# Output slices of the first block split as the others, the tail's counts moved forward, and a new order of the instructions

## The chip, the core and the metric

The kernel runs on one core of one Trainium2 chip. The metric is device time in microseconds (us) of one execution, taken on the chip. TensorE is called PE below, VectorE DVE, ScalarE ACT, GpSimd POOL, and SyncE, which issues most of the DMAs, SP.

## The reference, cut to what matters

Attention over 4 batches, 8 heads, 768 positions and 64 columns a head, in which a position sees the 96 positions behind it and 8 global ones, with a bias by distance; then a gated feed-forward of 3072 rows, 512 columns and 1536 hidden columns, whose weights come as float64.

```python
scores = scale * np.matmul(q, k.transpose(0, 1, 3, 2))
scores = scores + bias[None, :, :, :]
scores = np.where(keep, scores, -1000000000.0)
scores = scores - np.max(scores, axis=-1, keepdims=True)
a = np.exp(scores)
a = a / (np.sum(a, axis=-1, keepdims=True) + 1e-09)
attn_out = np.matmul(a, v).astype(np.float32)
...
x = np.ascontiguousarray(attn_out.transpose(0, 2, 1, 3)).reshape(B * S, H * D)
gate = 1.0 / (1.0 + np.exp(-(x @ w_gate)))
val = x @ w_val
return (gate * val @ w_out).astype(np.float32)
```

## The kernel before

The 3072 rows are eight blocks of three tiles of 128 rows. For block 0 the attention comes first; after that, the feed-forward of a block runs while the attention of the next is woven into it. A block's feed-forward is twelve slices (f0 to f11) of 128 hidden columns. `ff_in` makes a slice: twelve matmuls of 128x384 for the gate (`ps_g`), twelve for the value (`ps_u`), a tanh on ACT (L654), and the product on DVE. `ff_out` (L686) multiplies a slice with 512 columns of `w_out` for each of the three tiles, into three banks of PSUM that gather all twelve slices.

Float32 precision is had in two ways. A *split* operand is kept as a high part rounded to the type fp32r and a low part that is the rest; a product of two split operands is three fp32r matmuls (low x high, high x high, high x low). The gate and value matmuls are all of this kind (`w1h`, `w1l`, `xh`, `xl`). In `ff_out` it is so from slice f6 of block 0 on: the weights are split into `w2h` (ACT, L299) and `w2l` (a subtraction on POOL, L268) by `split_w2`, anew for each slice and into one buffer each; the hidden values into `hh` (ACT, L666) and `hl` (a subtraction on DVE, also recorded at L268). For the slices f0 to f5 of block 0, `UNSPLIT = 6`, DVE writes the product to `hh` at once (L660), nothing is split, and `ff_out` does one plain float32 matmul a tile, which stands in the trace as two records.

During block 0 the weights arrive: per slice two transfers of gate and value weights and one of `w_out`, as 64-bit numbers, from which ACT takes the mantissa bits (L280) and the top (L287), DVE joins them (L296; for `w_out` it also does the top, L289), ACT rounds `w1h` (L317) and POOL subtracts `w1l` in eight parts (L268).

The order of the instructions on each engine is written out by hand in the table `ORDER` for the first part of the program (on PE the first 1273 operations); what comes after is issued in the order that the scheduler chose. An engine runs its instructions in order, so one that waits holds up all behind it. SP's list sets the order of the transfers.

At the start PE does fourteen matmuls on zeros (`keep_busy`, L195), while the first q and k arrive and DVE builds the tables of distances (L220 to L230, L245). At the end the last tile is copied out of PSUM in halves, by DVE (L704) and then ACT (L705), and sent by a DMA of ACT's queue (L706). Behind `inner.close()` a check of the counts follows: the tiles `nf` and `wf` are allocated in `gpool`, in memory that was held by other tiles before; DVE computes them from `words` (L841 to L844), compares (L859, five times), reduces to one flag (L861), every engine loads the flag (L937) and branches (L938). The branch taken writes one element (L939); the other, a dense computation of everything anew, isn't run with these inputs.

Of the kernel before, what the change touches and what calls it, by code (L numbers as in the profile page):

```python
# [8 lines left out]
F32 = mybir.dt.float32  # L9
# [11 lines left out]
P = 128  # L21
# [86 lines left out]
def attn_moe_kernel(ctx, tc, qT, kT, v, counts, wg, wv, wo, out, B, H, S, D):  # L108
# [94 lines left out]
    make_identity(nc, ident)  # L203
    tabs = [cpool.tile([P, WIN], BF16, name=f"tab{h}") for h in range(H)]
    tabs0 = [cpool.tile([P, P], BF16, name=f"tabs{h}") for h in range(H)]
    nms = cpool.tile([P, 2 * (B * NTB * NPAIR) + 8], F32, name="nms")[:, :-8]
    def build_tables():

        nl, ng = low[:, 0:1], low[:, 1:2]
# [779 lines left out]
```

## Time and profile before

| | us |
|---|---|
| runs | 731.41, 732.67, 732.76 |
| median | 732.67 |
| profiled execution, its own time | 732.67 |
| its span | 730.9 |
| PE busy | 718.9 (98%) |
| DVE busy | 462.2 (63%) |
| ACT busy | 412.9 (56%) |
| POOL busy | 229.0 (31%) |

The span is the time from the first to the last record of the trace; the profiled execution's own time is 1.8 us above it. A share of busy time is an average over the whole program. The chain of waits is the sequence of work that ended last, followed back from the end; the view of windows gives busy time by stage; the waits of an engine name what it stood still for.

### The profile page before, as it was taken

What the parts mean: (1) busy time and instruction counts of PE and PEld (TensorE: products, weight loads), DVE (VectorE), ACT (ScalarE), POOL (GpSimd) and SP (SyncE); (2) the same over time, 40 slices, a digit from 0 to 9 for tenths busy, and PEclk for the clock granted to TensorE, in tenths of its full rate; (3) what the DMA queues carried; (4) which work ended last, traced back from release to release, by engine and by line L of the source; (5) the groups of instructions that cost most, each with busy time, mean ns of one, the idle gap of its engine ahead of it and who ended that gap; (6) DMA issues with size and microseconds to landing.
All of it is one profiled execution on the core that took longest, in us unless ns stands there. A gap on an engine that the chain in (4) does not pass through costs nothing.

```text
span 730.9 us, 12504 instructions
## 1 busy us (share of the span) xinstructions
PE 718.9 (98%) x4403; PEld 654.2 (90%) x4403; DVE 462.2 (63%) x1273; ACT 412.9 (56%) x938; POOL 229.0 (31%) x238
## 2 busy tenths in 40 slices
PE   8999999999999999999999999999999999999995
PEld 7777789989999899999999999999999999999994
DVE  6866664477777767777777777676787877221112
ACT  6777875656666545565565655565465755332222
POOL 4744665232322313232322223232223232212221
PEclk9999999999999999999999999999999999999998
DMA  7787542454354653444326343532335333010001
GB/s 236 237 285 266 190 154 79 110 106 89 84 137 84 149 102 69 98 117 96 61 64 146 77 107 75 89 102 63 91 82 111 87 61 56 15 44 1 1 0 47
DMA packets 136723, 74.27 MB, mean 102 GB/s; under 512 B 86992, under 2 KB 128976, under 8 KB 136656
## 3 DMA queue, kind: packets, MB, share of 16 engines
q1 hardware_dynamic: 136368, 73.17, 40.1%
q8 instruction: 36, 0.59, 0.3%
q14 instruction: 31, 0.25, 0.1%
q10 hardware_dynamic: 288, 0.26, 0.1%
HBM read 49.81 MB, written 6.29 MB: 77 GB/s over the span
## 4 chain that ended last, share of the span: by engine, by line
PE 95%; DMA 2%; DVE 1%; POOL 1%; ACT 1%; issue 0%; SPq 0%; DVEq 0%; ACTq 0%
PE ps_o L686 27%; PE ps_u L646 27%; PE ps_g L646 27%; PE ps_s L469 4%; PE ps_t L584 3%; PE ps_v L584 2%; PE ps_t L534 1%; PE ps_v L195 1%; DMA kr<-in_kT 1%; PE ps_s L455 1%; DMA turned<-halves 1%; POOL w2l L268 1%; PE ps_v L455 0%; DVE halves L549 0%; PE ps_o L610 0%
## 5 line engine op out<-in xcount | busy, mean ns | idle before, releaser
L268 POOL TENSOR_TENSOR w2l<-w2f,w2h 128x512 fp32r<-128x512 f32 x89 | 119.8, 1346 | 367.0 <-ACT w2h L299 361.2
L663 DVE SCALAR_TENSOR_TENSOR work<-work,ps_u 128x384 f32<-128x384 f32 x90 | 49.8, 553 | 140.9 <-PE ps_u L646 133.1
L646 PE MATMUL ps_g<-xh,w1l 128*128 128x384 f32 x384 | 131.8, 343 | 1.2 <-ACT work L654 1.2
L646 PE MATMUL ps_u<-xh,w1l 128*128 128x384 f32 x384 | 131.7, 343 | 0.2 <-DVE work L663 0.2
L646 PE MATMUL ps_g<-xl,w1h 128*128 128x384 f32 x384 | 130.0, 339 | 0.0
L646 PE MATMUL ps_g<-xh,w1h 128*128 128x384 f32 x384 | 129.7, 338 | 0.0
L646 PE MATMUL ps_u<-xl,w1h 128*128 128x384 f32 x384 | 129.3, 337 | 0.0
L646 PE MATMUL ps_u<-xh,w1h 128*128 128x384 f32 x384 | 129.3, 337 | 0.0
L666 ACT ACTIVATE hh<-work 128x384 fp32r<-128x384 f32 x90 | 47.0, 522 | 120.9 <-DVE work L663 120.6
L686 PE MATMUL ps_o<-w2l,hh 128*128 128x512 f32 x267 | 105.8, 398 | 0.8 <-POOL w2l L268 0.7
L686 PE MATMUL ps_o<-w2h,hh 128*128 128x512 f32 x267 | 103.9, 391 | 0.0
L686 PE MATMUL ps_o<-w2h,hl 128*128 128x512 f32 x267 | 103.3, 390 | 0.0
L501 ACT ACTIVATE work<-work,nms 128x256 f32<-128x256 f32 (+1 forms) x192 | 92.0, 481 | 12.4 <-DVE nms L488 11.8
L268 DVE TENSOR_TENSOR hl<-work,hh 128x384 fp32r<-128x384 f32 x90 | 73.3, 814 | 30.4 <-ACT hh L666 30.4
L299 ACT ACTIVATE w2h<-w2f 128x512 fp32r<-128x512 f32 x89 | 56.1, 631 | 59.0 <-PE ps_o L686 58.2
L646 PEld LDWEIGHTS ps_u<-xh,w1l 128*128 128x128 f32 x384 | 72.2, 188 | 5.1 <-issue 2.0
L646 PEld LDWEIGHTS ps_g<-xh,w1l 128*128 128x128 f32 x384 | 72.3, 188 | 4.8 <-ACT work L654 2.0
L654 ACT ACTIVATE work<-ps_g 128x384 f32<-128x384 f32 x96 | 46.6, 486 | 51.2 <-PE ps_g L646 48.4
L646 PEld LDWEIGHTS ps_g<-xl,w1h 128*128 128x128 f32 x384 | 72.2, 188 | 2.5 <-issue 1.1
L646 PEld LDWEIGHTS ps_u<-xl,w1h 128*128 128x128 f32 x384 | 72.2, 188 | 1.9 <-issue 0.2
L646 PEld LDWEIGHTS ps_g<-xh,w1h 128*128 128x128 f32 x384 | 72.2, 188 | 1.5 <-issue 0.5
L646 PEld LDWEIGHTS ps_u<-xh,w1h 128*128 128x128 f32 x384 | 72.2, 188 | 0.8
(125 smaller groups left out, 1178.9 us busy)
## 6 DMA issues: line engine op xcount, KB each, us to landing
qr<-in_qT SPq DMA_DIRECT2D x56, 192.0 KB, 3.4
kr<-in_kT SPq DMA_DIRECT2D x32, 192.0 KB, 2.7
raw<-in_w_gate SPq DMA_DIRECT2D x12, 512.0 KB, 4.8
raw<-in_w_val SPq DMA_DIRECT2D x12, 512.0 KB, 5.8
v<-in_v SPq DMA_DIRECT2D x32, 192.0 KB, 3.4
raw<-in_w_out SPq DMA_DIRECT2D x12, 512.0 KB, 4.0
out<-ost SPq DMA_DIRECT2D x23, 256.0 KB, 2.2
v<-in_v SPq DMA_DIRECT2D x16, 144.0 KB, 3.4
```

Source lines behind the costliest of these rows:

```text
L195: ins = nc.tensor.matmul(idle[:, 0:P], zeros.to_broadcast([P, P]), zeros.to_broadcast([P, P]), start=True, stop=True)
L268: eng.tensor_tensor(out, a, b, op=ALU.subtract)
L299: ins = nc.scalar.activation(hi, w, AF.Copy)
L455: ins = nc.tensor.matmul(ps[j][:, :w], st["qr"][hd, 0, qc], st["kr"][hd, k0:k0 + w], start=True, stop=True)
L469: nc.tensor.matmul(ps[j][:, :w], st["qs"][:, j, hl, qc], st["ks"][:, j, k0:k0 + w], start=(hl == 1), stop=(hl == 0),)
L501: ins = nc.scalar.activation(sb[:, j, :w], sb[:, j, :w], AF.Exp, scale=-1.0, bias=nm[:, j:j + 1], accum_out=sm[:, j:j + 1])
L584: ins = nc.tensor.matmul(av[j * D:(j + 1) * D, t * P:(t + 1) * P], vt[:, t, j * D:(j + 1) * D], st["pT"][t][:, m * j + c], start=(c == 0), ...
L646: nc.tensor.matmul(ps[:, :n], wt[f][:, i, c], xt[:, c, :n], start=(k == 0), stop=(k == 3 * NC - 1))
L654: last_gate[:] = [nc.scalar.activation(a[:, :n], ps[:, :n], AF.Tanh, scale=0.5)]
L663: nc.vector.scalar_tensor_tensor(a[:, :n], a[:, :n], 1.0, pss[1][:, :n], op0=ALU.add, op1=ALU.mult)
L666: nc.scalar.activation(hh[:, :n], a[:, :n], AF.Copy)
L686: ins = nc.tensor.matmul(outs[bi][t], ht[:, t * P:(t + 1) * P], wt, start=(f == 0 and k == 0), stop=(f == NF - 1 and k == len(parts) - 1),)
```

## The change

Four things change.

- `UNSPLIT` goes from 6 to 0: the slices f0 to f5 of block 0 split their weights and hidden values as all the others. Eighteen float32 matmuls become fifty-four fp32r ones; ACT gets six more `w2h` and six more `hh`, POOL six more `w2l`, DVE six more `hl`.
- `nf` and `wf` lie in eight spare columns of the tile `nms`, which is kept through the whole program. So their operations can stand in DVE's list near the start.
- The last tile is copied once, by ACT, and sent by ACT's queue as before.
- All five lists of `ORDER` are new; PE's names 1307 operations in place of 1273. Behind the lists, the order of PE, DVE, ACT and POOL is the same as before, up to the tail.

```diff
@@ ORDER
     tensor=(
-        "0-9 14-17 11 10 13 12 21 27 20 18-19 26 53 33 52 32 22 28-31 23-25 46-51 59 58 34 36-45 54-57 35 65 64 85 60-63 "
+        "0-9 14-15 11 13 10 21 12 20 18 16 19 27 22-23 33 26 53 32 24-25 28-31 17 46-52 59 58 36-45 34-35 54-57 85 65 64 "
...
-    nms = cpool.tile([P, 2 * (B * NTB * NPAIR) + 8], F32, name="nms")[:, :-8]
+    nms = cpool.tile([P, 2 * (B * NTB * NPAIR) + 8], F32, name="nms")
+    nf, wf = nms[:, -8:-6], nms[:, -6:].rearrange("p (w k) -> p w k", k=2)
+    nms = nms[:, :-8]
...
-    UNSPLIT = 6
+    UNSPLIT = 0
...
-                if t == nt - 1 and end:
-                    y, z = slice(0, DM // 2), slice(DM // 2, DM)
-                    nc.vector.tensor_scalar(ot[:, y], outs[bi][t][:, y], 0.5, None, op0=ALU.mult)
-                    nc.scalar.activation(ot[:, z], outs[bi][t][:, z], AF.Copy, scale=0.5)
-                    nc.scalar.dma_start(out[bass.ds(row, P), :], ot)
-                    continue
                 if t == 1 and end:
                     nc.vector.tensor_scalar(ot, outs[bi][t], 0.5, None, op0=ALU.mult)
                 else:
                     nc.scalar.activation(ot, outs[bi][t], AF.Copy, scale=0.5)
-                nc.sync.dma_start(out[bass.ds(row, P), :], ot)
+                (nc.scalar if end and t == nt - 1 else nc.sync).dma_start(out[bass.ds(row, P), :], ot)
...
-    nf = gpool.tile([P, 2], F32, name="nf")
-    wf = gpool.tile([P, 3, 2], F32, name="wf")
```

The table's numbers don't tell what moved; the orders do, at three places. In their rows a name carries the number of its buffer, and a line of after is 3 to 5 away from that of before.

PE at the start of the program, before: the matmuls on zeros (L195), then the first scores (L455) and transposes (L534).

```order
L195 MATMUL ps_v_100<-zeros_98 128x128 x14
L455 MATMUL ps_s_213<-kr_172,qr1_170 128x128
L455 MATMUL ps_g_214<-kr_172,qr1_170 128x128
L455 MATMUL ps_u_223<-kr_172,qr1_170 128x256
L455 MATMUL ps_o1_224<-kr_172,qr1_170 128x256
L455 MATMUL ps_s_243<-kr_172,qr1_170 128x256
L455 MATMUL ps_u_269<-kr_182,qr1_180 128x128
L455 MATMUL ps_g_244<-kr_172,qr1_170 128x256
L534 MATMUL ps_t_238<-ident_94,work_217 128x128 x2
```

The same place after.

```order
L198 MATMUL ps_v_100<-zeros_98 128x128 x12
L460 MATMUL ps_s_213<-kr_172,qr1_170 128x128
L460 MATMUL ps_u_223<-kr_172,qr1_170 128x256
L460 MATMUL ps_g_214<-kr_172,qr1_170 128x128
L460 MATMUL ps_s_243<-kr_172,qr1_170 128x256
L460 MATMUL ps_o1_224<-kr_172,qr1_170 128x256
L460 MATMUL ps_g_244<-kr_172,qr1_170 128x256
L539 MATMUL ps_t_238<-ident_94,work_217 128x128
L198 MATMUL ps_v_100<-zeros_98 128x128
L539 MATMUL ps_t_238<-ident_94,work_217 128x128
L460 MATMUL ps_u_269<-kr_182,qr1_180 128x128
```

Twelve matmuls on zeros stand ahead of the first scores in place of fourteen, and the scores of the second pair (`kr_182`) have moved behind the transposes of the first.

ACT about the first slices of block 0, before: the rounding of the weights (`w1h`), the tanh of f0 (`work_640`), the exponentials of the next block's attention (L501), and the bits of the next weights.

```order
L618 COPY hl_582<-ps_o2_575 128x384
L626 ACTIVATE xh_168<-hh_584 128x384
L280 ACTIVATE w2f1_157<-raw1_588 128x512
L317 ACTIVATE w1h1_133<-bits_597 128x1024
L654 ACTIVATE work_640<-ps_g_627 128x384
L501 ACTIVATE work_605,sm_606<-work_605,nms_131 128x256 x2
L514 ACTIVATE sm_606<-sm_606 128x2
L280 ACTIVATE bits_646<-raw0_593 128x1024
L287 ACTIVATE top_648<-raw0_593 128x1024
L501 ACTIVATE work_615,sm_616<-work_615,nms_131 128x256 x2
L317 ACTIVATE w1h2_134<-bits_646 128x1024
```

The same place after.

```order
L304 ACTIVATE w2h_677<-w2f0_156 128x512
L623 COPY hl_582<-ps_o2_575 128x384
L631 ACTIVATE xh_168<-hh_584 128x384
L322 ACTIVATE w1h1_133<-bits_597 128x1024
L285 ACTIVATE w2f1_157<-raw1_588 128x512
L506 ACTIVATE work_605,sm_606<-work_605,nms_131 128x256
L659 ACTIVATE work_640<-ps_g_627 128x384
L506 ACTIVATE work_605,sm_606<-work_605,nms_131 128x256
L519 ACTIVATE sm_606<-sm_606 128x2
L506 ACTIVATE work_615,sm_616<-work_615,nms_131 128x256
L671 ACTIVATE hh_673<-work_640 128x384
L285 ACTIVATE bits_646<-raw0_593 128x1024
```

The rounding of f0's `w_out` (`w2h_677`) now comes ahead of `w1h1`, and the rounding of its hidden values (`hh_673`) between the exponentials and the bits of f2.

DVE at the end of the program, before, from the last product on.

```order
L663 SCALAR_TENSOR_TENSOR work_8112<-work_8112,ps_u_8114 128x384
L268 TENSOR_TENSOR hl_8129<-work_8112,hh_8128 128x384
L709 TENSOR_SCALAR ost_8157<-ps_o1_7665 128x512
L704 TENSOR_SCALAR ost_8160<-ps_o2_7666 128x256
L841 CAST wf_8171<-words_91 128x2x2
L842 TENSOR_SCALAR wf_8171<-wf_8171 128x2
L843 TENSOR_TENSOR wf_8171<-wf_8171 128x2
L844 SCALAR_TENSOR_TENSOR nf_8170<-wf_8171 128x2
L859 TENSOR_SCALAR top_8176<-nf_8170 1x1 x4
L861 TENSOR_REDUCE flag_8186<-top_8176 1x1
L937 TENSOR_LOAD flag_8186
L938 COMPARE_AND_BRANCH
```

The same place after.

```order
L668 SCALAR_TENSOR_TENSOR work_8190<-work_8190,ps_u_8192 128x384
L273 TENSOR_TENSOR hl_8207<-work_8190,hh_8206 128x384
L708 TENSOR_SCALAR ost_8235<-ps_o1_7743 128x512
L934 TENSOR_LOAD flag_8261
L935 COMPARE_AND_BRANCH
```

The second copy of the last tile and the nine small operations are gone from here: four of the counts and four compares stand near the start, and the reduction to the flag (after L858) among the last block's slices. On SP the load of the flag stands ahead of the last five output transfers, and on ACT behind the last copy and its DMA.

## Rows read from the trace of the kernel before

**Rows 1.** The page: span, busy time by engine, and the chain's shares by engine.

```profile
span 730.9 us, 12504 instructions
PE 718.9 (98%) x4403; PEld 654.2 (90%) x4403; DVE 462.2 (63%) x1273; ACT 412.9 (56%) x938; POOL 229.0 (31%) x238
PE 95%; DMA 2%; DVE 1%; POOL 1%; ACT 1%; issue 0%; SPq 0%; DVEq 0%; ACTq 0%
```

**Rows 2.** The chain of waits from 715 us: start, duration, what.

```profile
723.04 0.43 DVE ost L704
723.50 0.39 ACT ost L705
723.92 2.06 DMA out<-ost
...
727.54 0.54 DVEq L937
...
728.24 0.54 issue
...
728.86 0.06 DVE top L939
```

**Rows 3.** The timeline from 719 us: start, duration, operation, idle before and releaser.

```profile
721.26 0.39 PE L686 MATMUL ps_o<-work,hl 128*128 128x512 f32 x1
...
721.68 0.60 ACT L711 ACTIVATE ost<-ps_o 128x512 f32<-128x512 f32 x1 [1.92 <-PE ps_o L686]
...
722.62 0.39 PE L686 MATMUL ps_o<-work,hl 128*128 128x512 f32 x1
...
726.20 0.17 DVE L841 CAST wf<-words 128x4 f32<-128x4 int32 x1 [2.73 <-DMA out<-ost]
```

**Rows 4.** The timeline of PE from 40 us: unsplit output matmuls, two records each.

```profile
40.95 1.02 PE L686 MATMUL ps_o<-w2f,hh 128*128 128x512 f32 x2
...
49.51 1.88 PE L686 MATMUL ps_o<-w2f,hh 128*128 128x512 f32 x4
```

**Rows 5.** The chain of waits from 290 us: nine split output matmuls in a row.

```profile
302.35 2.04 PE ps_o L686 x9
```

**Rows 6.** Windows: each engine's busy time (and its count), clock, DMA share, GB/s.

```profile
6.60:16.40 9.80, 9.05 (x78) 6.16 (x76) 7.72 (x36) 8.47 (x29) 5.34 (x8) 1.00 0.89 277
...
36.00:87.00 51.00, 51.00 (x278) 37.67 (x277) 31.78 (x77) 40.99 (x81) 27.00 (x54) 1.00 0.76 259
87.00:130.00 43.00, 43.00 (x259) 37.80 (x259) 24.73 (x60) 30.17 (x64) 24.24 (x36) 1.00 0.39 124
```

**Rows 7.** The page's costliest groups: the four operations that the split adds.

```profile
L268 POOL TENSOR_TENSOR w2l<-w2f,w2h 128x512 fp32r<-128x512 f32 x89 | 119.8, 1346 | 367.0 <-ACT w2h L299 361.2
...
L666 ACT ACTIVATE hh<-work 128x384 fp32r<-128x384 f32 x90 | 47.0, 522 | 120.9 <-DVE work L663 120.6
...
L268 DVE TENSOR_TENSOR hl<-work,hh 128x384 fp32r<-128x384 f32 x90 | 73.3, 814 | 30.4 <-ACT hh L666 30.4
L299 ACT ACTIVATE w2h<-w2f 128x512 fp32r<-128x512 f32 x89 | 56.1, 631 | 59.0 <-PE ps_o L686 58.2
```

**Rows 8.** Waits of ACT from 36 to 87 us: total, times, longest; first and last.

```profile
ACT w1h L317 <- DVE rc L518: 2.9, 2, 1.5
...
ACT bits L280 <- DMA raw<-in_w_val: 0.5, 1, 0.5
```

**Rows 9.** Waits of PE from 100 to 722 us: total, times, longest; two of three.

```profile
PE ps_g L646 <- ACT work L654: 1.2, 2, 0.8
PE ps_o L686 <- POOL w2l L268: 0.7, 2, 0.6
```

**Rows 10.** The chain of waits from the start to 36 us.

```profile
1.00 5.73 PE ps_v L195 x28
...
11.23 5.21 DMA kr<-in_kT
```

**Rows 11.** The view of the tile `hl`: shortest, median and longest subtraction in ns.

```profile
L268 DVE TENSOR_TENSOR hl<-work,hh x90: 543/559/1905, 84.8 to 719.8; 128x384 fp32r<-128x384 f32 x90
```

129 rows, old and new, of tables (gpsimd, scalar, sync, tensor) are left out of this document.

## The prediction

> **What bounds the kernel now.** I read the page first, then the chain of waits. PE is busy for 718.9 of 730.9 us and makes up 95% of the chain [rows 1]: between the first scores and the last output matmul nearly every saving must be one on PE itself, or a wait of PE that goes. Two places are different. At the end, the chain leaves PE at about 723.0 us and needs another 7.9 us for copies, one DMA, the check of the counts and a branch [rows 2]. At the start, 5.7 us are matmuls on zeros, and one transfer of k holds the chain until 16.4 us [rows 10]. So I take the change in three places (end, PE's work in block 0, start), and then ask which other engine is close enough to PE to spoil it. The windows show one: from 36 to 87 us, where block 0 runs f0 to f6 while the weights arrive, ACT is busy for 41.0 of 51.0 us, against 30.2 of 43.0 in the stretch behind [rows 6].
>
> The profiled execution took 732.67 us, which is the median of the three runs too; it is its span of 730.9 and 1.8 us around it. I sum against 732.67.
>
> **The end.** Before: the last matmul starts at 722.62; DVE copies one half at 723.04, ACT the other at 723.50 (0.39), the DMA goes at 723.92 and takes 2.06, to 725.98 [rows 2, 3]. Only then does DVE begin the counts: L841 sat idle for 2.73 us and its releaser is that DMA [rows 3], since `nf` and `wf` take over memory of the output tile. From there L841 to L861, the load of the flag (0.54), the branch (0.54) and L939 run to 728.92 [rows 2], and the span ends 2.0 us later at 730.9.
>
> After: one ACT copy. Tile 0's copy tells its price: its last matmul starts at 721.26, the copy at 721.68, and it takes 0.60 [rows 3]. So the copy runs from 722.62 + 0.42 = 723.04 to 723.64, the DMA goes at 723.67 and lands at 725.73, 0.25 earlier than before. The counts, the compares and the flag are long done. The loads of the flag and the branches stand behind the last work of each engine; ACT's are the latest: behind its DMA at 723.67 and some 0.4 us of issuing, 0.54 for the load and 0.6 for the branch make 725.2, half a microsecond before the landing. They are covered by the transfer; if that cover were gone, they'd cost up to 1.4 us. What is late next is the landing itself, and then the closing. Before, the closing took 2.0 us behind L939; if all of it comes behind the landing the span ends at 727.7 (a gain of 3.2), and if half of it has run by then at 726.7 (4.2). The chain of waits doesn't say what part waits for DMAs; I take 1.7 us, thus 727.4: **−3.5 us**, with 1.8 (loads and branches not covered) and 4.2 as ends.
>
> **PE's work in block 0.** An unsplit output matmul is two records. One takes 1.02 us, and two in a row 1.88 [rows 4], so one more costs 0.86. Nine split ones in a row take 2.04 us [rows 5], 0.227 each, and three of them 0.68. Eighteen matmuls thus save 18 x (0.86 − 0.68) = **−3.2 us**. All this lies on PE, which is the bound there (51.0 of 51.0 busy [rows 6]). The ends are 2.5 and 4.0, since single matmuls carry a change of operand shape in or out that the new order may add or save.
>
> **What the split adds elsewhere.** By the page's means [rows 7]: on ACT six times 0.631 + 0.522 = 6.9 us; on POOL six times 1.346 = 8.1; on DVE six times 0.814 = 4.9. In the window 36 to 87 us, which shrinks to 47.8, DVE comes to 31.8 + 4.9 = 36.7 and POOL to 27.0 + 8.1 = 35.1, both with more than 11 us to spare. ACT, with the first `w2h` ahead of the window (it stands in front of `w1h1`), comes to 41.0 + 6.3 = 47.3 of 47.8: full. It covers its extra work only by giving up its own waits. These were 10.2 us there in six rows, from 2.9 for DVE's `rc` to 0.5 for a transfer of weights [rows 8]. They are mostly the waits of an engine that is ahead, and PE didn't stand still behind them: it was busy for 51.00 of 51.00 us [rows 6]. Queued behind an ACT that waits are the tanh, on which PE's next gate bank depends, `hh`, on which the output matmuls depend, and `w1h`, on which POOL's `w1l` and PE's next slice depend. No row shows how much of this reaches PE. The bounds are 0 (all hidden, as before) and 47.3 + 10.2 − 47.8 = 9.7 us (no wait gives way). Behind 87 us ACT has 30% to spare and catches up. I take **+1.0**, near the lower end, since that is the nearest row: PE's waits for ACT after 100 us, where split slices run as well, are 1.2 us in all, in two waits [rows 9].
>
> **The start.** Two matmuls fewer on zeros ahead of the first scores are four records of 5.73/28 = 0.20 us, so up to 0.8 us earlier. PE is busy for 9.05 of 9.80 us between 6.6 and 16.4 [rows 6], so waits of 0.75 could go as well; the transfer of k that ended one at 16.4 was issued at 11.23 behind a 512 KB transfer of weights and took 5.2 [rows 10], and now it is issued ahead of that one. Against it: eight small DVE operations of 0.17 [rows 3] come in among the tables, 1.4 us at most, on which POOL's tables and the first softmax wait. Bounds −1.6 and +1.4; I take **−0.6**, as the new places of the scores and the transfers are on the side of the gain, and DVE has work for 7.72 of those 9.80 us.
>
> **The rest.** The two extra matmuls on zeros among the transposes, the new places of the same work in the lists, and the counts at the start change no amount of work; the order behind the lists is as before. I put them at nothing: where PE is never idle, order alone costs nothing (that PE comes some 4 us earlier to the later blocks is rival 2).
>
> Sum: 732.67 − 3.5 − 3.2 − 0.6 + 1.0 = 726.4 us.
>
> **Rival 1, slower: ACT becomes the bound from 36 to 87 us.** For it: 47.3 of 47.8 us with no room for a wait, in an order in which a wait for a transfer or for DVE's `bits` holds the tanh too. Against it: PE was busy for all of the 51.0 us while ACT waited 10.2, so ACT's lateness of that size was hidden by work done ahead, and such a lead is used up first. Its price is 9.7 us at most: 732.67 − 3.5 − 3.2 − 0.6 + 9.7 = 735.1. It decides the sign when over 7.3 of the 10.2 us of waits stay; with half of them, 5, the time is 730.4.
>
> **Rival 2: the later stalls grow.** PE arrives earlier at blocks whose transfers and POOL work are timed by others. Its waits from 100 to 722 us are 1.2 for ACT and 0.7 for POOL, and 0.2 more [rows 9]. As much again gives 726.4 + 2.1 = 728.5. Against it: the waits are single events, and PE was the bound around them.
>
> **Rival 3: POOL's subtractions block DVE's.** `hl` takes 0.559 us at the median and 1.905 at the longest [rows 11], and its mean of 0.814 [rows 7] says that a fifth or so of them are stretched by the 1.35 us between these two. POOL would be busy for 35.1 of 47.8 us in the window, so four of the six new `hl` may meet it: 5.4 us on DVE, which its spare 11 us can hold; if half of that reaches the matmuls that read `hl`, it is 2.7 and the time 729.1. The Trainium skill has the rule on the page "SBUF — State Buffer", section "Who interferes with whom": a DVE instruction with two inputs in SBUF and a GpSimd instruction that reads SBUF exclude each other, and the later one blocks fully. By that rule the cost of a meeting is the rest of the other's instruction, and the longest `hl` agrees with it.
>
> **Rival 4: the start or the end gives nothing.** If the eight operations and the new order of POOL's tables cost the start 1.4 us in place of the gain of 0.6, and the branches cost the end 1.0, the time is 726.4 + 2.0 + 1.0 = 729.4. The DMA's end behind the last matmul can't be gained away, but neither is it made longer.
>
> **How the numbers follow.** The forecast of 726.4, with its own ends at 723.4 (the large ends of the gains at the end and the start: 0.7 and 1.0, and no stall: 1.0, with 0.3 taken off since they won't all fall together) and 728: chance 0.62. Rival 1: 0.14, of which 0.04 lies above 734.1 and 0.04 between 731.2 and 734.1. Rival 2: 0.10. Rival 3: 0.07. Rival 4: 0.07. 0.2% of 732.67 is 1.5 us, about what a measurement of this kernel can tell from no change. Slower by more than that: 0.05 (rival 1, and a mixture of the others); within it: 0.05; faster: 0.90. The range reaches from 723.4 to 731.0, which leaves out the worse half of rival 1 and a start and end that are better than counted.
>
> **What would show it.** In the profile after: the last DMA's landing at about 718.5 on a span of 724.6, with no DVE operation behind it but L936, and 1.7 us to the end; the record count of `ps_o<-w2f,hh` at zero and PE busy for some 3 to 4 us less; the first scores near 6 us; ACT above 95% from 36 us to the end of f5, and PE's waits for ACT, `w1l` or `hl` before 90 us at about 1 us in all. I'm wrong if PE stands still for several microseconds in f0 to f6, if the closing waits for something that I don't see, or if the first scores don't move.

## The result: 723.55 us, 1.2% faster than before

The changed kernel took 723.55 us (median of four runs, 723.22 to 724.73); four runs of the kernel before beside it took 732.68 (731.41 to 732.76). The ratio is 0.9882, with a 95% interval of 0.9865 to 0.9899: faster by 9.1 us, where 6.3 were forecast. The time lies inside the range and close to its low end.

The page after: span, busy time by engine, and the four groups that the split adds to (a group is line, engine, operation, count | busy us, mean ns of one | idle time before, its releaser).

```profile
span 723.0 us, 12575 instructions
PE 714.1 (99%) x4421; PEld 659.1 (91%) x4421; DVE 467.2 (65%) x1278; ACT 418.3 (58%) x950; POOL 239.1 (33%) x244
...
L273 POOL TENSOR_TENSOR w2l<-w2f,w2h 128x512 fp32r<-128x512 f32 x95 | 129.4, 1363 | 370.8 <-ACT w2h L304 359.7
L671 ACT ACTIVATE hh<-work 128x384 fp32r<-128x384 f32 x96 | 50.1, 522 | 120.5 <-DVE work L668 120.2
L273 DVE TENSOR_TENSOR hl<-work,hh 128x384 fp32r<-128x384 f32 x96 | 77.8, 810 | 30.3 <-ACT hh L671 30.1
L304 ACT ACTIVATE w2h<-w2f 128x512 fp32r<-128x512 f32 x95 | 59.9, 630 | 56.9 <-PE ps_o L691 56.1
```

Each group has grown by six [rows 1, 7], at nearly the same price for one: ACT, POOL and DVE work 5 to 10 us longer, PE 4.8 us less. This execution took 724.73 us by its own time, the slowest of its four; a second profiled one (`again`, below) took 723.36, and where two executions of one kernel differ I show both.

### The profile page after: what moved, and what is told of

Read it like the earlier page. It is cut to its first block, busy times and chain, and to the rows that moved or that the text cites. A ratio compares the mean times of both kernels' runs of the same rounds, so it can differ in the third digit from the quotient of the medians.

```text
span 723.0 us, 12575 instructions
## 1 busy us (share of the span) xinstructions
PE 714.1 (99%) x4421; PEld 659.1 (91%) x4421; DVE 467.2 (65%) x1278; ACT 418.3 (58%) x950; POOL 239.1 (33%) x244
## 5 line engine op out<-in xcount | busy, mean ns | idle before, releaser
L273 POOL TENSOR_TENSOR w2l<-w2f,w2h 128x512 fp32r<-128x512 f32 x95 | 129.4, 1363 | 370.8 <-ACT w2h L304 359.7
L668 DVE SCALAR_TENSOR_TENSOR work<-work,ps_u 128x384 f32<-128x384 f32 x96 | 53.1, 553 | 137.8 <-PE ps_u L651 130.1
L671 ACT ACTIVATE hh<-work 128x384 fp32r<-128x384 f32 x96 | 50.1, 522 | 120.5 <-DVE work L668 120.2
L691 PE MATMUL ps_o<-w2l,hh 128*128 128x512 f32 x285 | 112.0, 395 | 1.1 <-ACT hh L671 1.0
L691 PE MATMUL ps_o<-w2h,hh 128*128 128x512 f32 x285 | 111.0, 391 | 0.0
L691 PE MATMUL ps_o<-w2h,hl 128*128 128x512 f32 x285 | 109.7, 391 | 0.0
L273 DVE TENSOR_TENSOR hl<-work,hh 128x384 fp32r<-128x384 f32 x96 | 77.8, 810 | 30.3 <-ACT hh L671 30.1
L304 ACT ACTIVATE w2h<-w2f 128x512 fp32r<-128x512 f32 x95 | 59.9, 630 | 56.9 <-PE ps_o L691 56.1
L659 ACT ACTIVATE work<-ps_g 128x384 f32<-128x384 f32 x96 | 46.6, 485 | 49.0 <-PE ps_g L651 48.6
```

The costliest lines, as they stand in the source:

```text
L273: eng.tensor_tensor(out, a, b, op=ALU.subtract)
L304: ins = nc.scalar.activation(hi, w, AF.Copy)
L659: last_gate[:] = [nc.scalar.activation(a[:, :n], ps[:, :n], AF.Tanh, scale=0.5)]
L668: nc.vector.scalar_tensor_tensor(a[:, :n], a[:, :n], 1.0, pss[1][:, :n], op0=ALU.add, op1=ALU.mult)
L671: nc.scalar.activation(hh[:, :n], a[:, :n], AF.Copy)
L691: ins = nc.tensor.matmul(outs[bi][t], ht[:, t * P:(t + 1) * P], wt, start=(f == 0 and k == 0), stop=(f == NF - 1 and k == len(parts) - 1),)
```

## Where the time went, by the traces

**The end.** The timeline of after from the last matmul on: start, duration, operation, idle before and releaser.

```profile
717.00 0.39 PE L691 MATMUL ps_o<-work,hl 128*128 128x512 f32 x1
717.42 0.60 ACT L710 ACTIVATE ost<-ps_o 128x512 f32<-128x512 f32 x1 [0.76 <-PE ps_o L691]
718.01 0.06 DVE L936 MEMSET top<- 1x1 f32 x1 [0.58 <-DVE ost L708]
718.05 0.37 ACTq L711 DMA_DIRECT2D out<-ost  x1
```

DVE has taken the branch and written its element at 718.01, before the last transfer is even issued; in [rows 2, 3] L939 came at 728.86, behind the transfer. One copy puts the transfer 1.05 us behind the last matmul in place of 1.30, the 0.25 that was forecast. From the last matmul's start to the end of the span it is 723.0 − 717.00 = 6.0 us, before it was 8.3. That is a gain of 2.3, not 3.5. The missing microsecond is in the transfer. From the views of the DMAs near the end, of before and then of after (issues: what, queue, count, KB each, median us from issue to landing):

```profile
out<-ost SPq DMA_DIRECT2D x2, 256.0 KB, 2.1
out<-ost ACTq DMA_DIRECT2D x1, 256.0 KB, 2.1
```

```profile
out<-ost SPq DMA_DIRECT2D x2, 256.0 KB, 3.0
out<-ost ACTq DMA_DIRECT2D x1, 256.0 KB, 3.3
```

The landing is at 721.35, and from there it is 1.6 us to the end of the span; 1.7 was taken.

**PE's stops.** The waits of PE from 5 us to the end, in after (who waited, for whom: total, times, longest):

```profile
PE ps_u L460 <- DMA kr<-in_kT: 1.0, 1, 1.0
PE ps_o L691 <- ACT hh L671: 1.0, 1, 1.0
PE ps_u L460 <- DVE sums L609: 0.2, 1, 0.2
```

The same view of `again`:

```profile
PE ps_u L460 <- DVE sums L609: 0.3, 1, 0.3
```

Before, the same view gives 2.9 us in five rows, the longest two of which are those of [rows 9]; neither is left. So 0.7 to 2.6 us of stops are gone, and two waits of 1.0 us come and go between executions of the same kernel.

**PE's own time.** The start of the last matmul, less that of the first scores, less the waits of that view, is PE's time for the work between. The first scores of before, after and `again`, and the last matmul of `again`:

```profile
6.66 0.37 PE L455 MATMUL ps_s<-kr,qr 64*128 64x128 f32 x1
6.09 0.48 PE L460 MATMUL ps_s<-kr,qr 64*128 64x128 f32 x2
6.46 0.70 PE L460 MATMUL ps_s<-kr,qr 64*128 64x128 f32 x2
715.49 0.39 PE L691 MATMUL ps_o<-work,hl 128*128 128x512 f32 x1
```

Before: 722.62 − 6.66 − 2.9 = 713.1 us. After: 717.00 − 6.09 − 2.2 = 708.7; in `again` 715.49 − 6.46 − 0.3 = 708.7 too. So 4.4 us are PE's own; the split was to give 3.2. The other traces agree: with before's order on PE and the clock at full speed it is 712.6 to 713.4 (before, and the tail alone, the counts alone and the one moved instruction below), with the whole change 708.7 to 708.9 (after, `again`, and three below that differ from after by one or two operations). The clock has no part in it: the granted clock reads 1.00 in before, after and the kernel without the split from the first matmul to behind 716 us. The experiments take split and order apart.

**The start.** The first scores come at 6.66 us before and at 6.09 and 6.46 after, near the 6 us forecast.

**ACT from 36 to 87 us.** The windows of `again`: engine busy time and count in the order PE, PEld, DVE, ACT, POOL, then granted clock, DMA share, GB/s.

```profile
36.00:87.00 51.00, 51.00 (x310) 44.09 (x309) 37.49 (x85) 46.94 (x94) 36.00 (x59) 1.00 0.85 274
```

ACT went from 41.0 us [rows 6] to 46.9 of 51.0 (which hold some 3 us more of the program than before), and PE is still busy for all 51.00. ACT's waits from 33 to 87 us, in `again`, are now these five, all for work that PE or DVE does just then:

```profile
ACT work L659 <- PE ps_g L651: 1.5, 3, 0.8
ACT w2h L304 <- PE ps_o L691: 0.8, 2, 0.4
ACT pT L544 <- PE ps_t L539: 0.7, 2, 0.4
ACT hh L671 <- DVE work L668: 0.5, 2, 0.3
ACT work L506 <- DVE nms L493: 0.4, 1, 0.4
```

The waits for `rc` and for transfers of weights, which stood at the ends of [rows 8], are gone; 10.2 us have become 3.9.

## The experiments

In a changed kernel, lines after an edit are a few off. Every ratio is to runs of the kernel before on the same chip. The runs below used four chips, and before's medians on them are 732.46, 732.10, 732.42 and 731.22 us, so a difference between medians of two chips is unsure by some tenths.

**The changed kernel again.** Without an edit.

> The changed kernel as it is, for a second trace of it beside the other runs. Theory A: the 1.2 us by which the last output DMA took longer in the first trace (3.30 us against 2.06) belong to that one execution, and so does the 1.0 us wait of PE for ACT hh; then the DMA takes 2.0 to 2.2 here, and the span behind the last matmul's start is near 4.8 us. Theory B: the shorter tail brings the last three transfers closer together, so the DMA takes over 3 us again and the tail 6.0.

723.58 us, ratio 0.9879 (0.9858 to 0.9900). The gain is there again; its trace is the second of after, used throughout.

**The tail alone.** Before, with the counts in `nms` and one copy.

```diff
+    nf, wf = nms[:, -8:-6], nms[:, -6:].rearrange("p (w k) -> p w k", k=2)
...
-                    nc.vector.tensor_scalar(ot[:, y], outs[bi][t][:, y], 0.5, None, op0=ALU.mult)
-                    nc.scalar.activation(ot[:, z], outs[bi][t][:, z], AF.Copy, scale=0.5)
```

> The kernel before with the change of the tail alone: counts in the kept tile, the last tile copied once by ACT, all lists as before. If the tail is worth what I forecast, 3.5 us less than before: 729.2. If the closing transfers collide as in the first trace of after, 2.3 less: 730.4. If the counts among the tables at the start cost PE time, up to 1.4 more than either.

729.29 us, ratio 0.9960 (0.9943 to 0.9977): 3.2 us faster, between 1.7 and 4.2. From the last matmul's start to the end of the span 5.8 us are left of 8.3, so its trace gives the tail 2.5; the rest of its 3.2 lies within the interval. Its last transfer takes 3.1 us.

**The split undone.** After, with the split of f0 to f5 taken back (each float32 matmul stands where the last of its three stood) and everything else kept.

```diff
-    UNSPLIT = 0
+    UNSPLIT = 6
```

> The changed kernel with the split of f0 to f5 in block 0 undone: the eighteen plain float32 matmuls are back, each where the last of its three stood, and the six w2h, hh, w2l and hl are gone; order and tail are those of after. Theory: the split is worth its saving on PE alone, since PE waits for nothing there in either kernel: 3.2 us slower than after, 726.7. Rival: the extra work on ACT and POOL cost something that doesn't show as a wait of PE; then less than 2.5 us slower.

727.05 us, ratio 0.9928 (0.9911 to 0.9944): 3.5 above after. Its first scores, its last matmul and the longest of PE's three waits (1.5 us in all):

```profile
5.77 0.48 PE L459 MATMUL ps_s<-kr,qr 64*128 64x128 f32 x2
718.62 0.39 PE L690 MATMUL ps_o<-work,hl 128*128 128x512 f32 x1
PE ps_o L690 <- ACT hh L670: 1.0, 1, 1.0
```

PE's own time, worked out as above, is 718.62 − 5.77 − 1.5 = 711.4 us. So the split gives 711.4 − 708.7 = 2.7 us of PE's time by the traces and 3.5 by the medians, with 3.2 forecast; as ACT's extra work goes with it, this is the split less what ACT's pressure may take from it. The other 713.1 − 711.4 = 1.7 come from the order, which I had put at nothing; set against all four traces of before's order it is 1.3 to 2.0.

Measured between the same output matmuls, and without the time in which PE stood idle, the 1.7 lie mainly in two places. From f6 of block 0 to f0 of block 1 (87 to 136 us of before) PE takes 49.5 us before, 48.6 with the split undone and 48.7 after. From f0 of block 2 to f0 of block 3 (225 to 318 us) it takes 92.3 before, 91.8 in the tail alone, and 91.3 with the split undone and after. From there to the last matmul all of them agree within 0.1.

**The late part of the order.** After, with the operations behind 143 us put back into before's relative order; and before, with those behind 147 us in after's.

```diff
@@ ORDER, all lists, from the operations at 143 us on
-        (after's order)
+        (before's relative order of the same operations)
```

> The changed kernel, but what its lists place behind 143 us of its trace stands in the relative order that it had before; the part ahead is untouched. Theory A: the order itself took away the stalls of PE between 150 and 250 us (about 2.4 us), so they come back here and the time is 725.9. Rival: they went because PE and ACT reach those places at another phase than before; then the time stays within 0.5 us of the changed kernel, 723.5.

> The kernel before (no split of f0 to f5, its own tail), in which only what its lists place behind 147 us of its trace now stands in the relative order of after. Theory A: the order there takes away the stalls of PE between 150 and 250 us; then 2.4 us faster than before, 730.1. Rival: they go by phase, that is by when PE comes there; then within 0.7 us of before, 732.5, with the stall of 0.9 us at 154 us in place.

The first took 726.10 us, ratio 0.9907 (0.9889 to 0.9926), 2.5 above after; the second 731.45, ratio 0.9990 (0.9981 to 1.0000), at most 1.4 us faster than before. PE's waits from 100 us on, first with the old late order in after, then with the new one in before:

```profile
PE ps_s L475 <- DVE nms L494: 1.5, 1, 1.5
PE ps_g L652 <- ACT work L660: 0.5, 1, 0.5
PE ps_o L692 <- POOL w2l L274: 0.2, 1, 0.2
```

```profile
PE ps_s L472 <- DVE nms L491: 0.9, 1, 0.9
PE ps_o L689 <- ACT hh L669: 0.2, 1, 0.2
```

Before's stops for the tanh (`work`) and `w2l` near 150 us, 1.0 us in all, come back with the old order (0.7) and are gone with the new one; they stand in the tail alone, the counts alone and the copy alone too, and in no trace with after's order. Before's other stops, 1.3 us between 200 and 250 us, don't come back with the old order, and of the kernels with before's lists only before and the counts alone have them in full: they come and go, and aren't the order's. PE's time from 225 to 318 us follows the order in both kernels: 92.2 us with the old late order, 91.3 with the new. But each kernel has a new stop for `nms` (from 259.9 and 149.6 us on) that stands in neither before nor after, and that I put down to my sewing two orders together. Without those the late part is worth 2.5 − 1.5 = 1.0 us by the one and 0.65 + 0.9 = 1.55 by the other. That it is about 1.0 to 1.6 us is my reading; the seam can't be taken out of the measurement.

**One stop, by one move.** At 152 us of before PE waits 0.8 us for a tanh (L654), which waits for DVE. DVE's timeline there, then POOL's:

```profile
151.61 0.62 DVE L268 TENSOR_TENSOR ks<-kr,ks 64x448 fp32r<-64x448 f32 x1
152.24 2.41 DVE L549 COPY halves<-work 128x512 int16<-128x512 int16 x2
```

```profile
152.28 2.10 POOL L268 TENSOR_TENSOR qs<-qr,qs 128x768 fp32r<-128x768 f32 x1 [3.72 <-ACT qs L427]
```

Two copies take 2.41 us beside a subtraction of POOL. I moved DVE's `ks` behind them, so that they come before POOL starts.

```diff
@@ ORDER, vector
-        221 206 219 220 212-213 234
+        221 206 219 212-213 220 234
```

> The kernel before with one DVE instruction moved: at 151.6 us the subtraction of ks, which stood ahead of the two copies to halves, stands behind them, so that both copies are issued before POOL's subtraction of qs begins at 152.3. Theory: a DVE copy that is issued while POOL subtracts is held until POOL is done (2.07 us in place of 0.3 to 0.4), and this is the stall of PE at 154 us; then the copies take 0.3 to 0.4 each, the waits of 0.8 (ACT tanh) and 0.2 (POOL w2l) go, and the time is 1.1 us less than before, 731.4. Rival: the copy is slow by itself or ACT's tanh is late for another reason; then no change.

731.98 us, ratio 1.0002 (0.9993 to 1.0011): nothing. DVE, then POOL, in this kernel:

```profile
152.22 0.76 DVE L550 COPY halves<-work 128x512 int16<-128x512 int16 x2
153.01 2.29 DVE L269 TENSOR_TENSOR ks<-kr,ks 64x448 fp32r<-64x448 f32 x1
```

```profile
152.97 1.85 POOL L269 TENSOR_TENSOR qs<-qr,qs 128x768 fp32r<-128x768 f32 x1 [3.72 <-ACT qs L428]
```

The copies take their 0.76 now, and the subtraction that took 0.62 takes 2.29: the collision has moved to the next instruction, and PE waits 0.7 us for the product (L664) in place of 0.8 for the tanh.

**The stop that comes and goes.** In after PE stands 0.98 us for `hh` at 183; in `again` it doesn't. (It does with one transfer fewer, with ACT loaded and with the split undone too, below and above, which all have this order here: four traces of five.) DVE, then POOL, in after:

```profile
181.40 1.39 DVE L554 COPY halves<-work 128x512 int16<-128x512 int16 x1 [0.31 <-DMA turned<-halves]
182.72 0.54 DVE L668 SCALAR_TENSOR_TENSOR work<-work,ps_u 128x384 f32<-128x384 f32 x1
```

```profile
181.22 1.30 POOL L273 TENSOR_TENSOR w2l<-w2f,w2h 128x512 fp32r<-128x512 f32 x1 [5.09 <-ACT w2h L304]
```

And in `again`:

```profile
180.74 0.43 DVE L554 COPY halves<-work 128x512 int16<-128x512 int16 x1
181.17 0.56 DVE L668 SCALAR_TENSOR_TENSOR work<-work,ps_u 128x384 f32<-128x384 f32 x1
```

```profile
180.82 1.51 POOL L273 TENSOR_TENSOR w2l<-w2f,w2h 128x512 fp32r<-128x512 f32 x1 [5.11 <-ACT w2h L304]
```

In `again` the copy starts 0.08 us before POOL's subtraction and takes 0.43; in after it waits 0.31 for a transfer, starts 0.18 behind POOL, and takes 1.39. The product behind it, `hh` and PE's matmul are late by the difference. The Trainium skill, page "SBUF — State Buffer", section "Who interferes with whom", has this as a rule: the engine that issues first holds the shared pair of ports for its whole instruction and the other blocks fully; it counts copies among DVE's instructions that can meet it. Both traces agree, 0.43 against 1.39.

So the product was put ahead of the copy; and in a second kernel SP also sends the global k of the first pair third in place of fifth, for the wait of 1.0 us at the start.

```diff
@@ ORDER, vector
-        293 295 294 290 298 299
+        293 295 294 298 290 299
@@ ORDER, sync (second kernel only)
-        1 0 7 6 2 12 8
+        1 0 2 7 6 12 8
```

> The changed kernel with one DVE instruction moved: at 181 us the product of the gate (which hh needs) stands ahead of the copy to halves. In the first trace of after that copy was issued 0.2 us behind the start of POOL's w2l and took 1.39 us, and PE then waited 1.0 us for hh; in the second it was issued 0.1 us ahead of it, took 0.43, and PE didn't wait. Theory: whichever of a DVE copy and a POOL subtraction starts first holds the other, and a few tenths decide; then PE has no wait for hh at 182 us here in any case, and the median is 0.3 to 0.7 us less than after: 723.0. Rival: the place is not on PE's path in most executions; then within 0.2 us of after, and the wait for hh may show again.

> As product_first, and on SP the small transfer of the first pair's global k (the fifth) stands ahead of the second pair's k and q. In the first trace of after it landed at 7.52 us and PE waited 1.0 us for it, in the second at 6.86, with no wait. Theory: it lands at about 5.7 here and the wait is gone in every execution; then another 0.2 to 0.6 us less, 722.6. Rival: the time is taken back at the next wait of the start (the sums on DVE, the second pair's k); then as product_first.

722.94 us, ratio 0.9867 (0.9853 to 0.9881), and 722.80, ratio 0.9865 (0.9851 to 0.9880). In the first the product runs at 181.62 and the copy after it takes 0.77, beside POOL; the wait for `hh` is gone, and PE's waits are 0.8 us in all, for the k. In the second they are these:

```profile
PE ps_u L462 <- DVE sums L611: 0.2, 1, 0.2
```

So the mechanism holds: both traces are without the stop. The second kernel is the fastest measured here, by its median 0.75 us below after; against after alone the intervals overlap too far to call that a difference, and the 0.14 us that the early k adds to the first move can't be told from nothing.

**ACT loaded on purpose.** After, with three copies of 128x256 behind each of the first six `w2h`, reckoned at 5.9 us of ACT in all.

```diff
+        if len(extra) < 6 * 3:
+            for _ in range(3):
+                extra.append(nc.scalar.activation(spare, w2f[f].bitcast(F32)[:, 0:DM // 2], AF.Copy))
```

> The changed kernel with three more ACT copies (128x256, to a spare tile that nobody reads) behind each w2h of f0 to f5: eighteen of some 0.33 us from start to start, 5.9 us, where ACT is busy for 37.3 of 39.7 us. If ACT is the bound there as rival 1 of the prediction has it, once its room is used: 3.5 us (beyond its room) to 5.9 us slower than after, 727.1 to 729.5, with waits of PE for ACT before 90 us. If the weights done ahead cover it: under 1 us slower.

728.07 us, ratio 0.9944 (0.9931 to 0.9958): 4.5 us slower than after. Its window, then PE's waits from 5 to 100 us without those for k:

```profile
36.00:87.00 51.00, 48.65 (x293) 40.70 (x291) 32.74 (x76) 48.85 (x102) 30.20 (x54) 1.00 0.76 251
```

```profile
PE ps_t L596 <- ACT pT L551: 1.1, 1, 1.1
PE ps_o L698 <- ACT sm L526: 0.4, 1, 0.4
PE ps_g L658 <- ACT work L666: 0.4, 1, 0.4
...
PE ps_o L698 <- POOL w1l L275: 0.2, 1, 0.2
```

PE is no longer busy all the time; it waits for ACT, and ACT is the bound. The copies are dearer than reckoned: by the trace they hold ACT for 0.40 us each from start to start, 7.3 us in all. Of these, 4.5 arrive in the time, so ACT's slack in after was about 2.8 us (in after's own trace it is idle for 2.4 of the 39.7 us of f0 to f5): rival 1's mechanism exists, and the change stopped short of it by that. And PE's own time is 711.2 us here, for 708.7 in after with the same matmuls. So the lateness of another engine can also lie in time in which PE counts as busy, where no wait shows it.

**Counts alone, the copy alone, and one transfer fewer.** Why does the last transfer take 3.3 us? The first kernel is before with the counts in `nms`, copies in halves as they were; the second is before with the one copy, and its counts still behind the landing; the third is after without the transfer of the last block's middle tile.

```diff
-                (nc.scalar if end and t == nt - 1 else nc.sync).dma_start(out[bass.ds(row, P), :], ot)
+                if not (end and t == 1):
+                    (nc.scalar if end and t == nt - 1 else nc.sync).dma_start(out[bass.ds(row, P), :], ot)
```

> The kernel before with the counts alone moved into the kept tile; the last tile is still copied in halves by DVE and ACT, and the lists are as before. If the whole gain of the tail is the counts, the load of the flag and the branch that no longer come behind the last DMA: 729.3 to 729.5, as tail_only (729.3). If the one copy by ACT gives its 0.25 us as forecast: 729.5. If two copies and a later DMA keep the last transfers further apart, so that the DMA takes 2.1 us as before: below tail_only, 728.5.

> The changed kernel without the output DMA of the last block's middle tile, so that those 128 rows are not written; all copies are made. Theory: the last DMA takes 3.0 to 3.4 us in after, against 2.06 before, since it is issued 0.5 us behind the middle tile's in place of 0.8 and the two share the DMA engines; then it takes 2.0 to 2.3 here and the time is 1.0 us less than after, 722.5. Rival: it takes longer because of something on ACT's own queue or because it is one copy; then over 2.9 us again and no change of time.

> The kernel before with one edit: the last tile is copied once by ACT (0.60 us) and sent by ACT's queue; the counts stay in the pool's memory, so that they, the flag and the branches still come behind the landing of the last output transfer. What is disputed is why that transfer takes 2.8 to 3.4 us in all kernels with early counts and 2.1 in the kernel before. Theory A (code): with early counts the engines branch while the transfer is under way, and the code that they then fetch (three packets of the instruction queue in the transfer's window, none in the kernel before) makes some of its last packets late. Here nothing branches before the landing, so the transfer takes 2.0 to 2.3 us, there is no instruction packet between its issue and its landing, and the copy gains its 0.25 us: 732.2 us, between 731.7 and 732.7. Theory B (neighbour): the transfer is longer since it is issued only about 0.6 us behind SP's one of the middle tile, in place of 0.84. Here it is as close to it as in the kernel with the whole change, so it takes 2.8 us or more, and the gain of the copy is lost: 732.8 us, up to 733.5.

Counts alone: 729.88 us, ratio 0.9963 (0.9951 to 0.9974), 2.5 of the 3.2 us that the tail gives; the last transfer takes 2.8, though it is issued 0.83 us behind SP's last one, as far as before. One transfer fewer: 723.31, ratio 0.9881 (0.9866 to 0.9896); the transfer takes 2.5. From the last matmul on this trace is 0.7 us shorter than after's, but the median is only 0.3 lower, which is within the noise; 1.0 was expected. The copy alone: 731.24 beside 731.22, ratio 1.0000 (0.9990 to 1.0009), so its 0.25 us don't show in the time; the transfer takes 2.1, though it is issued 0.59 us behind SP's last one, as in after, and not 0.84 as before. So a near neighbour alone doesn't make it longer, and early counts alone do; with both, in the tail alone, it takes 3.1. The DMA's windows about the last transfers, first of after (717 to 721.4 us), then of the copy alone (724 to 728): GB/s in 40 slices, and the queues with packets, MB and share.

```profile
GB/s 0 0 0 0 130 261 391 410 335 391 298 75 0 37 19 186 298 503 354 335 428 373 335 317 428 335 372 317 131 56 168 19 37 19 19 0 0 0 0 0
...
q14 instruction: 3, 0.02, 1.6%
```

```profile
GB/s 0 0 0 0 0 0 0 0 0 0 0 348 369 369 369 389 348 328 103 389 348 389 348 369 430 410 348 369 348 410 451 369 205 62 0 0 0 0 0 0
...
q1 hardware_dynamic: 288, 0.52, 34.8%
q10 hardware_dynamic: 144, 0.26, 17.2%
```

After has three packets of an instruction queue among the outputs, and the transfer ends in a thin tail: from 317 GB/s it falls to 19 over some 0.8 us. The copy alone has no such packet, and ends within 0.2 us. The same three packets stand beside the last transfer in the tail alone, the counts alone and with one transfer fewer (2.5 to 3.1 us), and none in the kernel before and the copy alone (2.1). They come when the engines take the branch, which early counts let them do while the outputs still move; the Trainium skill, page "Runtime: NRT & Kernel Launch", section "Instruction fetch mechanics", says that a taken branch to code that isn't loaded must fetch it by DMA first, and these packets agree. In before the packets of this queue come from 729.2 us on, 1 us behind the branches at 728.1, when all outputs have landed. Without them the neighbour costs nothing, beside them 0.3 (3.1 against 2.8) to 0.8 us (3.3 against 2.5). That the transfer is longer when the program's end runs beside it is shown; that it is the fetch that makes it so is read from these packets, and no run takes the fetch apart from the branch. How packets of 8 KB make a few others so late, no run here shows either.

The profiled execution of the copy alone is the slowest of its eleven, 734.48 us. In its trace PE stands still for 0.4 us at 6.6 and for 1.1 us at 8.1; the granted clock then falls to 0.50, the lower of its two levels (1.2 GHz in place of 2.4), from 11.6 to 18.5 us, though PE is busy there all the time, and PE's own time is 715.8 us in place of 712.6 to 713.4. In the thirteen other traces it reads 1.00 up to the last matmul. By the last transfers it reads 1.00 here too, so the reading of these stands.

## Why the prediction was right, and by how much it was off

It named the sign, the places and the bound, and its sum was 2.8 us too high. That the time lies inside the range is in part luck. The low end has a slip: 726.4 − 0.7 − 1.0 − 1.0 is 723.7, and 0.3 taken off the gains, as its reason says, makes 724.0 and not 723.4; 723.55 lies below that. And errors made up for each other: the end gave about 1 us less than forecast by the traces, the charge of 1.0 for ACT wasn't needed, and the order, put at nothing, gave about 2. By terms, with the measured size from the traces and, where one run isolates it, from the medians:

| term | forecast | traces | medians |
|---|---|---|---|
| end | −3.5 | −2.2 to −2.6 | −3.2 |
| PE's split | −3.2 | −2.7, with ACT's pressure in it | −3.5, with ACT's pressure in it |
| ACT pressure | +1.0 | no wait of PE | |
| start (first scores) | −0.6 | −0.2 to −0.6 | |
| order: PE's time | 0 | −1.7 (−1.3 to −2.0) | |
| order: PE's stops | 0 | −0.7 to −2.6 | |
| start and order together | −0.6 | −3.0 (after), −4.5 (`again`) | −2.2 |

The last row's median is 727.05 − 729.29, the split undone against the tail alone; with the tail's 3.2 and the split's 3.5 it makes 8.9, and 9.1 and 8.9 were measured. The traces add up as well: 2.3 + 2.7 + 3.0 = 8.0 for after, whose profiled execution is 7.9 us below that of before, and 2.2 + 2.7 + 4.5 = 9.4 for `again`, with 9.3. Both sums close by the way in which they are made, so they test no term. Traces and medians come from different executions, and single stops of a microsecond come and go between these, so no term is known to better than about a microsecond.

**The end** was right in its mechanism: counts out of the path, loads and branches covered by the transfer, 0.25 us from the one copy (in the trace; the copy alone shows nothing of it in the time), 1.6 behind the landing for 1.7. The step that failed is the price of the transfer, taken from [rows 2] at 2.06, with "neither is it made longer" in rival 4. It is, by 1.2 us: it is longer in all ten traces in which the branches run beside it, by 0.4 to 1.3 us, and in none of the other four. Their cover has a price, most likely that of the code that they fetch. (The landing "at about 718.5" was a slip: by the sum it is 1.7 us ahead of the span's end at 724.6, thus 722.9. It came at 721.35 of 723.0.)

**The split** was right in mechanism and size: no record of `ps_o<-w2f,hh` is left, and 2.7 to 3.5 us stand against 3.2.

**ACT** gave up its waits, as said, but took less than was summed: in the 47.8 us from 36 us on with which the prediction reckoned, it is busy for 44.1 in after (92%), not 47.3, and from 33.5 to 73.2 us, f0 to f5, for 94%, not over 95%. No wait of PE for it shows there. The +1.0 can't be told from the split, since undoing the split takes ACT's extra work away too: for the two together −2.2 was forecast, and −2.7 to −3.5 was measured. The row that I took it from was the wrong neighbour: of the two waits for ACT after 100 us [rows 9], the one of 0.8 belongs to the order of that stretch and went with it, and the other comes and goes. **Rival 1** was priced fairly, since 7.3 us more of ACT, with 2.4 to 2.8 of slack, cost 4.5.

**"Order alone costs nothing"** is the step that failed most. PE was busy for all of 36 to 87 us, but not everywhere: its 2.9 us of stops were in the view that I had read, and I asked only whether they would grow (**rival 2**), not whether the new lists remove them. And busy isn't the same as fast: the same matmuls (and two on zeros more), in another order, take 1.7 us less of PE's time beside its waits, 0.9 of it from 87 to 136 us and most of the rest from 225 to 318. By what, I can't show.

**Rival 3** was right about the lock, wrong in the place. `hl` was no longer on the mean than before (810 ns against 814 [rows 7]); what blocked PE by 1 us was a copy with one input at 181 us, well behind the new work. **Rival 4** happened by half: the branches cost the end its 1.0 us and somewhat more, though through the transfer and not behind it. The start lost nothing, though the first scores scatter: the copy alone has the start of before and made its 28 records of zeros in another time,

```profile
1.00 5.20 PE L195 MATMUL ps_v<-zeros 128*128 128x128 f32 x28 [1.00 <-DVE zeros L189]
```

0.53 us less than in [rows 10]. (In both traces these records start 0.21 us apart until a moment, then 0.11, and the moment isn't the same.) A gain of 0.6 at the start can't be told from that in one trace. Over all fourteen the first scores come at 6.13 to 7.09 us with before's start, 6.68 on the mean of six, and at 5.77 to 6.46 with after's, 6.25 on the mean of eight: 0.4 us earlier.

## What to carry to other kernels

Where a change brings a new order, don't put the order at zero because the bound engine is busy: list that engine's waits in every stretch, and ask of each whether the new order keeps it. Work moved under a transfer isn't free: the branches moved under this one brought instruction packets to the DMA engines, and it took 0.4 to 1.3 us longer. An engine that fills up gives back its own waits first, so a load of 7 us on an engine with 10 us of waits cost nothing that shows, while 7.3 more cost 4.5. And undoing a change takes back all that it adds, so it can't tell a gain from a cost that comes with it.

## What the runs showed of the hardware that I had not expected

The last 256 KB transfer took 2.1 us in the four traces in which nothing branches before its landing, and 2.5 to 3.4 in the ten with instruction packets beside it, in after with a thin tail at the end. In one execution stops of 0.4 and 1.1 us at the start were followed by 7 us at half the clock. A start 0.08 us ahead of POOL or 0.18 us behind it decides whether DVE's copy of 128x512 takes 0.43 or 1.39 us, and so whether PE stops for 0.98 us. Moving one such instruction out of the way moved the collision to the next: 2.41 us for two copies became 2.29 for a subtraction, with no gain.
